# VectorE writes one element into both PSUM banks of a spectral step, and its eight products follow one another

## The chip, the cores and the metric

The kernel runs on one core of a Trainium2 chip. The metric is the device time of one execution in microseconds (us). TensorE is called PE in the profile, VectorE DVE, ScalarE ACT, GpSimd POOL, and SyncE SP; PEld is TensorE's loading of weights.

## What is computed

Eight sequences of 3072 positions and 256 channels pass three layers. The first is a filter in the frequency domain; the second and third are dense.

```python
X = np.fft.rfft(x, axis=1)                        # x: 8 x 3072 x 256, fp32
y = np.fft.irfft(X * (filt_r + 1j * filt_i), n=3072, axis=1)
prev = y shifted by one position
xk, xr = mu_k * y + (1 - mu_k) * prev, mu_r * y + (1 - mu_r) * prev
k = np.maximum(xk @ w_k, 0.0)                     # 256 -> 1024
z = sigmoid(xr @ w_r) * (k * k @ w_v)             # 1024 -> 256
h = np.maximum(np.maximum(z @ w1, z @ w2), z @ w3)  # 256 -> 768
out = h @ w_out                                   # 768 -> 256
```

## The kernel before

The **dense layers** are the main stream of the program. It takes 384 positions at a time. `k_mm` and `r_mm` multiply by `w_k` and `w_r`, `v_mm` by `w_v`; `block` does the maximum of three products for two such tiles at once with seven products in place of eight (tiles `pa`, `pb`, `pe`, line 850 on), and `o_mm` the last product (`po`). Each value is held as a sum of two parts, so that a product is three passes of 128x128 weights over 384 columns. ScalarE and VectorE read the banks out, and ScalarE, VectorE and GpSimd make the two parts.

The **transform** of sequence 0 runs ahead of all (`fft_first`). For sequences 1 to 7 `fft(b)` gives a list of small pieces, and `drive` deals them out among the main stream of the sequence before, by weight. A first part (`a_mm`, tile `pa<-xah,wa_s`) makes 24 groups of frequencies. The second part works on four groups at a time, so there are six values of `u` (`NU4`, line 29), and for each one `b_mm` (line 538: the transform's second stage, tile `pb<-xb,wbc`, then the filter) and one `c_mm` (line 559: the way back, tile `pc<-yz,wbc`). That is 12 steps for a sequence and 84 in all.

Each such **step** calls `quarters` (line 515). It takes two banks of the accumulator (PSUM) as `p[0]` and `p[1]`, and makes eight products with 64x64 weights over 256 columns. A product is named by `y`, `x` and `k`: `y` is the half of the 128 rows that the weights stand in, and also which of the two banks is written; `x` is the half of the columns and so of the bank's partitions; `k` is the half of the bank's 512 elements. The four places (`y`, `x`) of TensorE's array can work at the same time. A product is in full fp32, and the trace has two records of it, so that a step of eight products is 16 records.

All banks come from one **pool** of eight (`ps`, tag `pm`, line 261), for the main stream and the transform alike. A bank is taken again when its last reader is done, and whoever writes it first waits for that reader.

What sets the **order** on each engine: a scheduler plays the program through while it is built, with estimated times, and takes for an engine, of those instructions that it thinks ready, the one that stands first by priority. The products of `quarters` are written under `tc.high_priority()` and go ahead of the main stream as soon as the scheduler thinks them ready. Only the first part (`fft_first`, and SyncE's queue there) has an order by hand. On the chip each engine then works through its own fixed order, and waits on semaphores.

After `b_mm`'s products, for each bank: ScalarE copies the two halves of its partitions crosswise (lines 548, 549), VectorE multiplies by the filter (lines 550 to 552), and GpSimd does the rest (553, 555). After `c_mm`'s products ScalarE copies each bank out (line 566) and sends it to memory.

Of the kernel before, what the change touches and what calls it, by code (L numbers as in the profile page):

```python
# [11 lines left out]
I32 = mybir.dt.int32  # L12
U32 = mybir.dt.uint32
AF = mybir.ActivationFunctionType
ALU = mybir.AluOpType

N = 3072
# [12 lines left out]
H = NK // 2  # L30
# [175 lines left out]
def as_float(bits):  # L206
    return float(np.uint32(bits).view(np.float32))
# [29 lines left out]
def tile_spectral_moe(ctx: ExitStack, tc, x, xr, xz, filt, ones, wa, wa1, wi, wbc, wb1, wc1, filt1, filt0, mu, w_k, w_v, w_r, w1, w2, w3, w_out, out):  # L237
    nc = tc.nc
# [22 lines left out]
    ps = ctx.enter_context(tc.tile_pool(name="ps", bufs=8, space=bass.MemoryType.PSUM))  # L261

    def mm(o, wgt, rhs, start, stop, more=False, at=None):
        nc.tensor.matmul(o, lhsT=wgt, rhs=rhs, start=start, stop=stop, skip_group_check=more, tile_position=at)  # L264

    def mm3(o, parts, rhs_parts, onto=False, more=False):


        n = len(parts)
        for k in range(n):  # L270
            (wh, wl), (xh, xl) = parts[k], rhs_parts[k]
            mm(o, wh, xh, k == 0 and not onto, False, more)
            mm(o, wh, xl, False, False, more)
            mm(o, wl, xh, False, k == n - 1, more)
# [11 lines left out]
    def load_small():  # L286
        nc.scalar.dma_start(wi_s, wi)
        nc.scalar.dma_start(mu_s, mu)
        nc.vector.tensor_scalar(nmu_s, mu_s, -1.0, 1.0, op0=ALU.mult, op1=ALU.add)

    def split(hi, lo, src, lo_eng=None):
        nc.scalar.copy(hi, src)  # L292
        (lo_eng or nc.gpsimd).tensor_tensor(lo, src, hi.bitcast(F32), ALU.subtract)  # L293

# [3 lines left out]
    def piece(src, kt, t0, t1, c0, c1, parts):  # L298
# [18 lines left out]
        def narrow(late=True):  # L317
# [7 lines left out]
            ef = e.bitcast(F32)  # L325
            nc.scalar.activation(ef, high.bitcast(F32), AF.Abs)
            nc.vector.tensor_scalar(ef, ef, as_float(0x38000000), as_float(0x47EFFFFF), op0=ALU.max, op1=ALU.min)
            nc.vector.tensor_scalar(e, e, 3, 0x3FFFFFFF, op0=ALU.logical_shift_left, op1=ALU.bitwise_and)
            nc.vector.scalar_tensor_tensor(e, high, -0x40000000, e, ALU.bitwise_and, ALU.bitwise_or)
            m = fp.tile([P, a, c], I32, tag="fin", name="wm")  # L330
            mf = m.bitcast(F32)
            nc.vector.tensor_scalar(m, e, -0x800000, None, op0=ALU.bitwise_and)
            nc.vector.scalar_tensor_tensor(mf, low.bitcast(U32), 2.0**-52, mf, ALU.mult, ALU.mult)
# [106 lines left out]
    def fft(b):  # L440
# [73 lines left out]

        def quarters(o, of):

            for k in range(2):
                for y in range(2):
                    for x in range(2):
                        w, d = of(y, x, k)  # L520
                        with tc.high_priority():
                            mm(o[y][x * H : x * H + H, k], w, d, k == 0, True, True, (y * H, x * H))

        def b_load(u):
            w = fp.tile([NK, 2, 2, 2, H], F32, tag="fhi", name="wbc", bufs=3)
# [12 lines left out]
        def b_mm(u):  # L538
            w, f, t = st.pop(("b", u))
            p = [ps.tile([NK, 2, C], F32, tag="pm", name="pb") for _ in range(2)]  # L540
            quarters(p, lambda y, x, k: (w[y * H : y * H + H, 0, x, k], t[y * H : y * H + H, 2 * x + k]))
            y = []
            for z in range(2):
                fr, fi, q = f[z][:, 0], f[z][:, 1], p[z]
                v = fp.tile([NK, 2, C], F32, tag="flo", name="v", bufs=3)
                a, e, m = slice(0, NM), slice(NM, H), NM
                lo, hi = slice(H, H + NM), slice(H + NM, NK)
                nc.scalar.mul(v[lo], q[hi], sg_s[hi])
                nc.scalar.mul(v[hi], q[lo], sg_s[lo])
                nc.vector.scalar_tensor_tensor(fi[a], q[e], -1.0, fi[a], ALU.mult, ALU.mult)  # L550
                nc.vector.tensor_tensor(fi[e], q[a], fi[e], ALU.mult)
                nc.vector.tensor_tensor(fr, q, fr, ALU.mult)
                nc.gpsimd.tensor_tensor(fi[H:], v[H:], fi[H:], ALU.mult)
                yz = fp.tile([NK, 2, C], F32, tag="fin", name="yz")
                nc.gpsimd.tensor_tensor(yz, fr, fi, ALU.add)
                y.append(yz)
            st["c", u] = w, y

        def c_mm(u):
            w, t = st.pop(("c", u))  # L560
            p = [ps.tile([NK, 2, C], F32, tag="pm", name="pc") for _ in range(2)]
            quarters(p, lambda y, x, k: (w[y * H : y * H + H, 1, x, k], t[x][y * H : y * H + H, k]))
            sv = s2.rearrange("h m r g c -> (h m r) g c")
            for y in range(2):
                o = fp.tile([NK, 2, C], F32, tag="fo", name="co")
                nc.scalar.copy(o, p[y])
                g = 4 * u + 2 * y
                nc.scalar.dma_start(sv[:, g : g + 2, :], o)
# [211 lines left out]
    def r_mm(i):  # L780
        xh, xl = cs.pop(("r", i))
        g = mp.tile([P, 2, NT], F32, tag="gate", name="gate", bufs=3)
        for h in range(2):
            p = ps.tile([P, NT], F32, tag="pm", name="pr")
            s = slice(h * P, (h + 1) * P)
            mm3(p, [(wr[0][:, k, s], wr[1][:, k, s]) for k in range(2)], [(xh[:, k], xl[:, k]) for k in range(2)])
            nc.scalar.activation(g[:, h], p, AF.Sigmoid)
        cs["g", i] = g

    def k_mm(i, f):  # L790
# [4 lines left out]
        r = mp.tile([P, NT], F32, tag="kr", name="kr")  # L795
        nc.scalar.activation(r, p, AF.Relu)  # L796
        nc.vector.scalar_tensor_tensor(r, p, 0.0, r, ALU.max, ALU.mult)  # L797
# [247 lines left out]
    for p in range(1, NPAIR):  # L1045
        i = 2 * p + 2
# [85 lines left out]
```

## Time and profile before

| | us |
|---|---|
| time, median of 3 runs | 3199.36 (3198.39 to 3200.33) |
| the profiled execution | 3202.59 |
| its span, first to last instruction | 3200.7 |
| TensorE busy | 3119.8 (97%) |
| TensorE loading weights | 2966.4 (93%) |
| ScalarE busy | 1924.2 (60%) |
| VectorE busy | 1889.7 (59%) |
| GpSimd busy | 1740.4 (54%) |

The span is cut into stretches below: from 684 us to 850 us, for one, the steps of a sequence's transform run beside the main stream, and from 850 us to 1067 us there are none. This repeats some 383 us apart until 2766 us. The clock that TensorE was granted is given as a share of full speed. A timeline row gives the start, how long the row's merged instructions took from first start to last end, and their count; a matmul's record overlaps the next one's, so the distance of two starts, not the length, tells what a matmul takes from the engine's time. An entry in brackets at the end of a row is idle time ahead of it and what ended it.

### The profile page before, as it was taken

The numbers are of one execution on the slowest core, as the hardware profiler recorded it, in microseconds if no ns is written. First come the engines' busy times: TensorE is split into PE (matmuls) and PEld (weight loads), VectorE is DVE, ScalarE is ACT, GpSimd is POOL, SyncE is SP. The second block draws the span as 40 slices with busy tenths as digits, with TensorE's granted clock in tenths as the row PEclk, the third lists the DMA queues.
The fourth block names the chain that finished last, engine by engine and source line by source line (L and its number), as shares of the span: only waits on it lengthen the run. The fifth ranks groups of instructions, "written<-read, shape, count | busy, mean of one in ns | idle before, by whom it ended". The sixth has DMA issues, their size and how long they took to land.

```text
span 3200.7 us, 56204 instructions
## 1 busy us (share of the span) xinstructions
PE 3119.8 (97%) x19508; PEld 2966.4 (93%) x19508; DVE 1889.7 (59%) x3050; ACT 1924.2 (60%) x3968; POOL 1740.4 (54%) x1499
## 2 busy tenths in 40 slices
PE   6799999999999999999999999999999999999998
PEld 4799989999999999998999989999899999999998
DVE  4866666456665566555665466655665556555554
ACT  5556656566565565656666566665656566555554
POOL 3545655456564565545665455655655456444443
PEclk8799999999999999999999999999999999999999
DMA  9668667756777666856668576775777766555554
GB/s 293 225 219 283 201 221 251 205 172 206 242 237 201 189 199 211 268 174 201 218 216 242 168 221 202 255 215 166 225 222 242 197 180 204 172 172 159 167 167 122
DMA packets 388953, 666.64 MB, mean 208 GB/s; under 512 B 41760, under 2 KB 153408, under 8 KB 388032
## 3 DMA queue, kind: packets, MB, share of 16 engines
q1 hardware_dynamic: 323376, 588.23, 60.2%
q10 hardware_dynamic: 64576, 72.45, 6.5%
q8 instruction: 158, 2.59, 0.3%
q0 software_dynamic: 720, 2.36, 0.2%
q14 instruction: 123, 1.01, 0.1%
HBM read 577.03 MB, written 85.85 MB: 207 GB/s over the span
## 4 chain that ended last, share of the span: by engine, by line
PE 86%; DVE 6%; DMA 3%; ACT 2%; issue 2%; POOL 1%; SPq 0%; ACTq 0%; POOLq 0%; DVEq 0%
PE pb L264 20%; PE pk L264 13%; PE pv L264 13%; PE po L264 13%; PE pe L264 9%; PE pa L264 6%; PE pr L264 4%; PE py L264 4%; PE pc L264 2%; DVE sc L829 1%; DVE x L293 1%; PE ps L264 1%; DMA ws<-wud 1%; DVE kr L797 1%; POOL klo L293 1%
## 5 line engine op out<-in xcount | busy, mean ns | idle before, releaser
L264 PE MATMUL pb<-x,ws 128*128 128x384 f32 x3456 | 751.8, 338 | 3.8 <-DMA ws<-wud 2.3
L293 POOL TENSOR_TENSOR hh<-m,hh 128x384 fp32r<-128x384 f32 x384 | 407.2, 1069 | 616.6 <-ACT hh L292 509.7
L293 POOL TENSOR_TENSOR klo<-kr,khi 128x384 fp32r<-128x384 f32 x492 | 521.3, 1067 | 291.8 <-ACT khi L292 249.4
L264 PEld LDWEIGHTS pb<-x,ws 128*128 128x128 f32 x3456 | 598.4, 188 | 19.7 <-issue 8.4
L797 DVE SCALAR_TENSOR_TENSOR kr<-pk,kr 128x384 f32<-128x384 f32 x512 | 282.0, 553 | 451.8 <-ACT kr L796 450.4
L264 PE MATMUL pv<-khi,ws 128*128 128x384 f32 x2048 | 487.9, 340 | 13.5 <-ACT khi L292 13.4
L264 PE MATMUL po<-wo_hi,hh 128*128 128x256 f32 x2304 | 489.3, 284 | 2.7 <-ACT hh L292 2.0
L264 PEld LDWEIGHTS po<-wo_hi,hh 128*128 128x128 f32 x2304 | 392.1, 189 | 21.2 <-issue 9.6
L292 ACT CAST khi<-kr 128x384 fp32r<-128x384 f32 x512 | 262.1, 513 | 218.0 <-DVE kr L797 197.8
L264 PE MATMUL pe<-x,ws 128*128 128x384 f32 x1728 | 389.9, 338 | 0.0
L264 PEld LDWEIGHTS pv<-khi,ws 128*128 128x128 f32 x2048 | 361.6, 189 | 25.5 <-ACT khi L292 19.1
L264 PE MATMUL pk<-xh,wk_hi 128*128 128x384 f32 x1024 | 340.7, 337 | 3.9 <-ACT xh L292 3.3
L264 PE MATMUL pk<-xl,wk_hi 128*128 128x384 f32 x1024 | 344.3, 336 | 0.3 <-DVE xl L293 0.3
L264 PE MATMUL pk<-xh,wk_lo 128*128 128x384 f32 x1024 | 343.7, 336 | 0.0
L796 ACT ACTIVATE kr<-pk 128x384 f32<-128x384 f32 x512 | 249.6, 490 | 109.6 <-POOL klo L293 53.4
L264 PE MATMUL po<-wo_lo,hh 128*128 128x256 f32 x1152 | 315.5, 281 | 0.0
L264 PE MATMUL pv<-klo,ws 128*128 128x384 f32 x1024 | 305.5, 341 | 6.9 <-POOL klo L293 6.0
L264 PEld LDWEIGHTS pe<-x,ws 128*128 128x128 f32 x1728 | 298.2, 188 | 11.1 <-issue 9.6
L912 DVE TENSOR_TENSOR m<-sc,m 128x384 f32<-128x384 f32 x384 | 296.5, 775 | 8.1
L292 ACT CAST hh<-m 128x384 fp32r<-128x384 f32 x384 | 193.8, 514 | 152.6 <-DVE m L912 81.8
L293 POOL TENSOR_TENSOR xl<-xm,xh 128x768 fp32r<-128x768 f32 x126 | 231.3, 1854 | 91.6 <-ACT xh L292 91.5
L865 ACT COPY v<-pb 128x384 f32<-128x384 f32 x288 | 138.6, 481 | 175.7 <-PE pb L264 164.6
(129 smaller groups left out, 5777.1 us busy)
## 6 DMA issues: line engine op xcount, KB each, us to landing
ws<-wud SPq DMA_DIRECT2D x864, 256.0 KB, 3.4
ws<-wvd SPq DMA_DIRECT2D x512, 256.0 KB, 3.6
filt<-in_filt SPq DMA_DIRECT2D x84, 512.0 KB, 5.2
ws<-wud SPq DMA_DIRECT2D x288, 128.0 KB, 3.1
xz<-in_xz SPq DMA_DIRECT2D x56, 512.0 KB, 5.3
cin<-s SPq DMA_DIRECT2D x128, 192.0 KB, 4.3
out_dram<-osb ACTq DMA_DIRECT2D x192, 128.0 KB, 3.3
xr<-in_xr SPq DMA_DIRECT2D x56, 384.0 KB, 5.1
```

Of the source, the lines that this page charges most:

```text
L264: nc.tensor.matmul(o, lhsT=wgt, rhs=rhs, start=start, stop=stop, skip_group_check=more, tile_position=at)
L292: nc.scalar.copy(hi, src)
L293: (lo_eng or nc.gpsimd).tensor_tensor(lo, src, hi.bitcast(F32), ALU.subtract)
L796: nc.scalar.activation(r, p, AF.Relu)
L797: nc.vector.scalar_tensor_tensor(r, p, 0.0, r, ALU.max, ALU.mult)
L829: eng.tensor_tensor(t, a, b, ALU.subtract)
L865: nc.scalar.copy(st[to], st[of])
L912: nc.vector.tensor_tensor(m, c, m, ALU.max)
```

## The change

`mm` returns its instruction. `quarters` first has VectorE copy one element into each of the two banks, into the partition at which the row half `y` of the bank begins; the element comes from the data of that half's last product (`of(y, 1, 1)`), so that the copy also waits for that data. The second copy is kept behind the first. Then the eight products are made with `y` = 1 ahead of `y` = 0 for each `k`, and each is tied behind the one before it. `ORDER_ONLY` binds the scheduler's order and adds no semaphore. The copies stand outside of `tc.high_priority()`. The element that they write is overwritten by the products.

```diff
+ORDER_ONLY = mybir.DependencyInfo(mybir.DependencyClass.NoSync, mybir.DependencyReason.DATA)
@@
     def mm(o, wgt, rhs, start, stop, more=False, at=None):
-        nc.tensor.matmul(o, lhsT=wgt, rhs=rhs, start=start, stop=stop, skip_group_check=more, tile_position=at)
+        return nc.tensor.matmul(o, lhsT=wgt, rhs=rhs, start=start, stop=stop, skip_group_check=more, tile_position=at)
@@
         def quarters(o, of):
 
+            last = None
+            for y in range(2):
+                _, d = of(y, 1, 1)
+                i = nc.vector.tensor_copy(o[y][y * H : y * H + 1, 0, :1], d[:1, :1])
+                if y:
+                    tc.add_manual_dep(i.ins, last, ORDER_ONLY, reason="banks")
+                last = i.ins.name
+            last = None
             for k in range(2):
-                for y in range(2):
+                for y in (1, 0):
                     for x in range(2):
                         w, d = of(y, x, k)
                         with tc.high_priority():
-                            mm(o[y][x * H : x * H + H, k], w, d, k == 0, True, True, (y * H, x * H))
+                            i = mm(o[y][x * H : x * H + H, k], w, d, k == 0, True, True, (y * H, x * H))
+                        if last is not None:
+                            tc.add_manual_dep(i.ins, last, ORDER_ONLY, reason="quarters")
+                        last = i.ins.name
```

What this moves, first on TensorE, in a step of `b_mm` for sequence 2 (the names with a number are single tiles: `pb_7901` is the step's `p[0]`, `pb_7902` its `p[1]`; `pb1`, `pa1` and `pe1` are the main stream's banks). Before:

```order
L264 MATMUL pe1_7883<-x2_7560,ws_7805 128x384 [waits DMAHW0_49,DVE_49]
L264 MATMUL pe1_7883<-x2_7560,ws_7805 128x384 x2
L264 MATMUL pb_7901<-xb_7630,wbc_7628 64x256 [waits DVE_49]
L264 MATMUL pb_7901<-xb_7630,wbc_7628 64x256 x3
L264 MATMUL pb1_7831<-x2_7557,ws_7777 128x384 [waits Activation_49]
L264 MATMUL pb1_7831<-x2_7557,ws_7777 128x384 x2
L264 MATMUL pb_7902<-xb_7630,wbc_7628 64x256 [waits DVE_49]
L264 MATMUL pb_7902<-xb_7630,wbc_7628 64x256 x3
L264 MATMUL pb1_7875<-x2_7549,ws_7793 128x384 [waits Activation_49]
```

The four products of the first bank and the four of the second stand apart, with three products of the main stream between them. The same step on TensorE in the changed kernel (here `pb_7927` is `p[0]`, `pb_7928` is `p[1]`):

```order
L265 MATMUL pe1_7865<-x2_7590,ws_7811 128x384 [waits DVE_49]
L265 MATMUL pe1_7865<-x2_7590,ws_7811 128x384 x2
L265 MATMUL pb1_7901<-x2_7573,ws_7819 128x384 [waits Activation_49]
L265 MATMUL pb1_7901<-x2_7573,ws_7819 128x384 x2
L265 MATMUL pa1_7902<-x2_7576,ws_7842 128x384 [waits DMAHW1_49]
L265 MATMUL pa1_7902<-x2_7576,ws_7842 128x384 x2
L265 MATMUL pb1_7988<-x2_7566,ws_7866 128x384 [waits DMAHW3_49,Activation_49]
L265 MATMUL pb1_7988<-x2_7566,ws_7866 128x384 x2
L265 MATMUL pb_7928<-xb_7654,wbc_7652 64x256 [waits DVE_49]
L265 MATMUL pb_7928<-xb_7654,wbc_7652 64x256
L265 MATMUL pb_7927<-xb_7654,wbc_7652 64x256 x2
L265 MATMUL pb_7928<-xb_7654,wbc_7652 64x256 x2
```

The eight stand together now, and only the first waits. What it waits for is the second copy on VectorE, which stands in this place of VectorE's order (`gate` is `x2`'s product, `m` and `sc` belong to `block`):

```order
L916 TENSOR_TENSOR m_7871<-pe1_7865,v_7852 128x384 [waits Activation_49]
L830 TENSOR_TENSOR gate_7593<-pv_7705,gate_7593 128x384 [waits PE_49]
L830 TENSOR_TENSOR gate_7593<-pv_7706,gate_7593 128x384 [waits PE_49]
L521 COPY pb_7927<-xb_7654 1x1 [waits DMAHW0_49,DVE_49]
L521 COPY pb_7928<-xb_7654 1x1 [waits DMAHW4_49,DVE_49]
L923 TENSOR_TENSOR sc_7915<-pe1_7909,v_7894 128x384 [waits PE_49,Activation_49]
```

The two copies are new, and stand behind two additions to `gate` that do not belong to the step. The next step, one of `c_mm`, on VectorE (`pc_8083` is `p[0]`, `pc_8084` is `p[1]`):

```order
L521 COPY pc_8083<-yz_7689 1x1 [waits DVE_49]
L916 TENSOR_TENSOR m_8064<-pe1_8058,v_8032 128x384 [waits PE_49,Activation_49]
L924 TENSOR_TENSOR m_7871<-sc_8002,m_7871 128x384 [waits DVE_49]
L521 COPY pc_8084<-yz_7689 1x1 [waits Activation_49]
L920 TENSOR_TENSOR m_8018<-pa1_8051,m_8018 128x384 [waits PE_49]
```

and on TensorE:

```order
L265 MATMUL pb1_8050<-x2_7581,ws_7971 128x384 [waits Activation_49]
L265 MATMUL pb1_8050<-x2_7581,ws_7971 128x384 x2
L265 MATMUL pe1_8058<-x2_7590,ws_7990 128x384 [waits DVE_49]
L265 MATMUL pe1_8058<-x2_7590,ws_7990 128x384 x2
L265 MATMUL pc_8084<-yz_7680,wbc_6480 64x256 [waits DVE_49]
L265 MATMUL pc_8084<-yz_7689,wbc_6480 64x256
L265 MATMUL pc_8083<-yz_7680,wbc_6480 64x256
```

Two instructions of the main stream stand between the two copies here, and three products of `pe1_8058` between the read of `pe1_8058` by `m_8064` and the step. Over the whole program, TensorE's order before has the eight products of a step in two pieces of four in 42 of the 84 steps (six of each sequence's twelve); in 26 more they stand together, all four of one bank ahead of all four of the other, and in 16 together with the banks mixed. In the changed kernel they stand together in all 84. VectorE has 168 instructions more.

## Rows read from the trace of the kernel before

**Rows 1.** Page, busy time by engine, and granted clock in 40 slices.

```profile
PE 3119.8 (97%) x19508; PEld 2966.4 (93%) x19508; DVE 1889.7 (59%) x3050; ACT 1924.2 (60%) x3968; POOL 1740.4 (54%) x1499
...
PEclk8799999999999999999999999999999999999999
```

**Rows 2.** Busy time by stretch, with steps (684, 1067) and without (850).

```profile
core 0: us, PE busy (x) PEld busy (x) DVE busy (x) ACT busy (x) POOL busy (x), PEclk, DMA share, GB/s
...
684.00:850.00 166.00, 163.91 (x1073) 148.71 (x1072) 104.83 (x169) 104.62 (x208) 97.08 (x83) 1.00 0.67 210
850.00:1067.00 217.00, 216.90 (x1343) 214.22 (x1343) 122.73 (x201) 132.96 (x283) 121.52 (x105) 1.00 0.70 214
1067.00:1232.00 165.00, 162.91 (x1067) 147.72 (x1067) 104.90 (x167) 103.67 (x208) 96.84 (x82) 1.00 0.67 210
```

**Rows 3.** Timeline of TensorE, a step in two pieces: start, us, engine, operation, count.

```profile
708.88 0.69 PE L264 MATMUL pe<-x,ws 128*128 128x384 f32 x3
709.49 1.08 PE L264 MATMUL pb<-xb,wbc 64*64 64x256 f32 x8
710.50 0.79 PE L264 MATMUL pb<-x,ws 128*128 128x384 f32 x3
711.22 1.08 PE L264 MATMUL pb<-xb,wbc 64*64 64x256 f32 x8
712.23 0.79 PE L264 MATMUL pb<-x,ws 128*128 128x384 f32 x3
712.86 0.33 PE L264 MATMUL pa<-x,ws 128*128 128x384 f32 x1
```

**Rows 4.** Timeline of TensorE, a step together, one bank's four products first.

```profile
350.65 0.68 PE L264 MATMUL pe<-x,ws 128*128 128x384 f32 x3
351.17 0.68 PE L264 MATMUL pb<-x,ws 128*128 128x384 f32 x3
351.79 1.11 PE L264 MATMUL pb<-xb,wbc 64*64 64x256 f32 x16
352.82 0.38 PE L264 MATMUL po<-wo_hi,hh 128*128 128x256 f32 x1
353.05 0.28 PE L264 MATMUL po<-wo_lo,hh 128*128 128x256 f32 x1
353.17 0.28 PE L264 MATMUL po<-wo_hi,hh 128*128 128x256 f32 x1
```

**Rows 5.** Timeline of TensorE, a step together, banks mixed.

```profile
377.09 0.34 PE L264 MATMUL pk<-xl,wk_hi 128*128 128x384 f32 x1
377.35 1.10 PE L264 MATMUL pc<-yz,wbc 64*64 64x256 f32 x16
378.38 0.44 PE L264 MATMUL pk<-xh,wk_lo 128*128 128x384 f32 x1
378.66 0.33 PE L264 MATMUL pk<-xh,wk_hi 128*128 128x384 f32 x1
```

**Rows 6.** Timeline of TensorE, the first and the last of 42 steps in pieces.

```profile
367.93 1.08 PE L264 MATMUL pb<-xb,wbc 64*64 64x256 f32 x8
...
369.60 1.08 PE L264 MATMUL pb<-xb,wbc 64*64 64x256 f32 x8
...
2757.99 1.08 PE L264 MATMUL pc<-yz,wbc 64*64 64x256 f32 x8
...
2763.66 1.08 PE L264 MATMUL pc<-yz,wbc 64*64 64x256 f32 x8
```

**Rows 7.** Waits of TensorE, 684 to 850 us: total, times, longest.

```profile
PE pv L264 <- ACT khi L292: 1.3, 1, 1.3
PE pv L264 <- POOL klo L293: 0.8, 1, 0.8
```

**Rows 8.** Timeline of TensorE, the one step ahead of which it waited.

```profile
409.96 0.65 PE L264 MATMUL pc<-yz,wbc 64*64 64x256 f32 x4 [0.46 <-DVE filt L552]
412.07 1.98 PE L264 MATMUL pc<-yz,wbc 64*64 64x256 f32 x12 [1.46 <-DVE filt L552]
```

**Rows 9.** Groups of VectorE: count, busy us, mean ns, idle before.

```profile
L912 DVE TENSOR_TENSOR m<-sc,m 128x384 f32<-128x384 f32 x384 | 296.5, 775 | 8.1
...
L289 DVE TENSOR_SCALAR nmu_s<-mu_s 128x4 f32<-128x4 f32 x1 | 0.2, 169 | 7.4 <-DMA mu_s<-in_mu 7.4
```

**Rows 10.** Timeline of VectorE ahead of the step in rows 3.

```profile
707.37 1.02 DVE L818 TENSOR_TENSOR gate<-pv,gate 128x384 f32<-128x384 f32 x2 [3.43 <-PE pv L264]
708.31 0.55 DVE L908 TENSOR_TENSOR m<-pa,m 128x384 f32<-128x384 f32 x1
708.77 0.55 DVE L904 TENSOR_TENSOR m<-pe,v 128x384 f32<-128x384 f32 x1
```

## Prediction

> **What bounds the kernel now.** I read the busy times first. TensorE is busy for 97% of the span, the others for 54 to 60%, and its granted clock is full after the first slices [rows 1]. The stretches tell whether that holds where the change works: beside a transform TensorE is busy for 163.9 of 166 us, and without one for 216.9 of 217 [rows 2]. So it is TensorE's own order that sets the end, in both kinds of stretch, and in a stretch with twelve steps only about 2.1 us of waiting are to be had, 1.3 and 0.8 us on the main stream's `pv` products [rows 7]. None of it is a wait of the steps. What a step takes of TensorE's time is therefore worth its full length at the end of the program, up or down.
>
> The timelines of TensorE then give the price of a step. The reader has to look at distances of starts. A plain product takes 0.173 us (three from 350.65 to 351.17) and a `po` product 0.12 (353.05 to 353.17) [rows 4].
>
> - In two pieces [rows 3]: from 708.88 to 712.86 there are two pieces of four products (8 records each) and nine plain ones. 3.98 - 9 x 0.173 = 2.42 us, so 1.21 us a piece. That includes what is lost at its edges: 0.61 us from 708.88 to 709.49 for three plain products where 0.52 is usual, and as much again behind it.
> - Together [rows 4]: from 351.17 to 353.05 there are three plain products, the 16 records and one `po`. 1.88 - 0.52 - 0.12 = 1.24 us.
> - Together with the banks mixed [rows 5]: from 377.09 to 378.66, two plain products and 16 records. 1.57 - 0.35 = 1.22 us.
>
> So four products cost as much as eight. The eight run on four places of the array, two places for each `y`, and a piece has one `y` alone: half of the array stands idle in it.
>
> **The change, part by part.**
>
> *Joining the pieces.* Before, 42 of the 84 steps are in two pieces, the first and the last of them in [rows 6]. Each goes from 2.42 to 1.24 us, which gives 1.18 us, and 42 x 1.18 = 49.6 us. The changed order has all 84 together. The order inside the eight is a new one, with `y` = 1 first and two by two. Two other orders differ by 0.02 us [rows 4, 5], so I take nothing for that; 42 x 0.02 = 0.8 us bounds it. The 42 steps that were together already stay what they are.
>
> The Trainium skill says otherwise of one thing: TensorE: Matmul & The Clock Gate, Part 3, The mechanism, has matmuls start and end in strict program order. By that rule the order in the step told first, four of one `y` and then four of the other, would take as long as two pieces, and the 26 such steps would gain from the new order as well. The trace disagrees: 16 records of that order took 1.11 us from first start to last end [rows 4], no longer than the mixed ones' 1.10 [rows 5].
>
> *The copies.* 84 x 2 = 168 new instructions of VectorE on one element. The trace has none like them. The nearest row is the 128x4 operation with 169 ns [rows 9], which I take: 168 x 0.169 = 28.4 us of VectorE's time. VectorE is busy for 104.8 of 166 us where they fall [rows 2], so 24 x 0.169 = 4.1 us a stretch find room in its own time. From below the cost at the end is nothing, if TensorE has other work while they run; from above it is the whole 28.4, if TensorE stands through each of them.
>
> The Trainium skill has a rule against such copies: VectorE: DVE Perf Modes, Two Vector instructions with no wait between them, holds back an instruction whose partitions begin in another quadrant until all earlier ones are done. In the trace neighbours on VectorE do overlap, 708.31 and 708.77 start 0.46 us apart and take 0.55 each [rows 10]; with that 0.09 lost at each copy it would be 168 x 0.26 = 43.7 us of VectorE's time. No run here shows a copy held in this way.
>
> *The new wait.* Before, the first product of each bank waited for that bank's last reader. Now the eight wait for the second copy, and that for all that stands ahead of it on VectorE, which is strictly in order. The price is what VectorE needs from its last meeting with TensorE to the copy, less what TensorE has to do in the same time. In the first step shown, `m_7871` must be done before `pe1_7865`'s last three products. TensorE then has twelve plain products ahead of the step, 12 x 0.173 = 2.08 us. VectorE has two additions to `gate`, 1.02 us together [rows 10], and two copies, 0.34 us: 1.36 us, covered with 0.7 to spare. In the second step, after `m_8064` TensorE has three products, 0.52 us, plus the 0.09 at the edge. VectorE has an `m` of 0.55 to 0.78 us [rows 9, 10] and one copy of 0.17, together 0.72 to 0.95: TensorE stands for 0.1 to 0.3 us. I went through the twelve steps of this sequence in the changed order in this way: nine are covered with 0.3 us or more, two come out even, and one is the step just told. That is 0.1 to 0.5 us for a sequence, 7 x 0.3 = 2 us in all. Where a copy waits for ScalarE to free a bank, the order does not tell how late that is; I allow as much again. Together 4 us.
>
> Queued behind a waiting copy on VectorE is the main stream: `m`, `sc`, `kr`. ScalarE and then TensorE wait for these. VectorE's cover for that is the 61 us it is idle in a stretch of 166.
>
> *The banks.* The first bank is now taken, and stays empty, until the second is free as well. Before, its four products ran meanwhile. That costs nothing as long as the main stream finds enough of the other six banks, and the scheduler has placed main-stream products there; in the second step shown, two instructions of VectorE stand between the two copies. The other edits (the return value, the binding without a semaphore) add no instruction.
>
> *The sum.* The profiled execution took 3202.6 us. 3202.6 - 49.6 + 4 = 3157.0. It stands 3.2 us above the median of the runs, 3199.4, so for the median I take 3153.8, and forecast 3154.
>
> **The rivals.**
>
> *VectorE comes late throughout.* The scheduler's estimate of VectorE is too short, and TensorE stands for both copies at every step. Then all of the 28.4 us are lost: 3199.4 - 49.6 + 28.4 = 3178. For it speaks that the first product had to wait for nothing like this before; against it that in all the steps shown but the one told next [rows 8] TensorE never stood ahead of a step, though those waits were placed by the same scheduler.
>
> *The banks run short, and the kernel is slower.* TensorE stands while a first bank is kept for its partner. The place is the 42 steps that were in pieces, whose second bank came late: 1.73 us after the first in one of them (709.49 to 711.22) [rows 3], 5.67 in the last [rows 6]. If TensorE stood for the smaller of these in each, 42 x 1.73 = 72.7 us would be lost: 3199.4 - 49.6 + 72.7 = 3222.5. It is slower than before from 49.6 / 42 = 1.18 us a step on. For it speaks the one step in the trace that TensorE stood for, 0.46 and 1.46 us [rows 8]; against it that VectorE and ScalarE have 40% of idle time to free banks in, and that TensorE's changed order has plain products ahead of each step.
>
> *The eight don't run side by side.* They stand together in the order, but a product with `y` = 0 starts only when those with `y` = 1 are done, so that a step costs two pieces less two edges. Edges are some 0.2 us of a piece; 42 x 0.2 = 8.4 us would be won and about 4 lost to waits, and the 42 steps that are together now would lose: 42 x 0.98 = 41 us, as 2.42 - 0.2 - 1.24 = 0.98. That is 3236. Neither of the two orders of the eight in the trace did this [rows 4, 5].
>
> *The program-order rule holds after all,* and 26 more steps gain 1.18 us each: 30.7 us more, 3123. The trace is against it [rows 4].
>
> *A wash:* waits of 0.5 to 0.65 us a step over all 84, from VectorE's queue and from banks together, take 42 to 55 us, and the time stays within 0.2% (6.4 us, about what a measurement of this kernel can tell from no change).
>
> **How the numbers follow.** Forecast 0.76; VectorE late throughout 0.13; a wash 0.04; banks short 0.04; the eight not side by side 0.02; program-order rule 0.01. The forecast's own range is 3144 to 3164: up by 10 us of waits more, down by the waits that may go, 2 us of each stretch and 3.5 us around the step that waited [rows 8]. To leave out no more than 2 in 10 the range goes up to the rival with VectorE's copies and the 4 us on top of it: 3144 to 3182. Faster by over 0.2%: 0.76 + 0.13 + 0.01 = 0.90. Same 0.04. Slower 0.06.
>
> **What would show it.** The timelines after should have no piece with 8 records of `wbc`, and 84 rows with 16 that take 1.1 us; TensorE's busy time should fall by some 50 us, to about 3070, with its instructions unchanged, and its idle time in a stretch with steps should stay below 4 us. VectorE's groups should have 168 copies with a mean under 0.2 us. If the forecast fails by waits, rows of `wbc` carry a bracket with the copy's line behind the arrow (VectorE late) or the main stream's do with the readers of banks (banks short). If a row of 16 takes 2 us, the eight don't run side by side. The forecast rests most on TensorE's waits staying small: 0.6 us a step would undo it.

## The result, and the profile after

The changed kernel takes 3170.09 us (median of four runs, 3169.33 to 3171.45), and the kernel before, beside it, 3199.79 us (3198.39 to 3200.33). The ratio is 0.9913, 95% interval 0.9900 to 0.9925: 29.7 us faster. The forecast was 3154, so the sign is right and the time is 16 us above it. It lies inside the stated range, 3144 to 3182, but 6 us above the forecast's own range, 3144 to 3164; only the part that was added for the rival "VectorE comes late throughout" takes it in.

The page's busy times of the changed kernel, to be read against [rows 1]:

```profile
PE 3073.5 (97%) x19508; PEld 2938.0 (93%) x19508; DVE 1910.6 (60%) x3218; ACT 1913.8 (60%) x3968; POOL 1746.8 (55%) x1499
```

Its profiled execution took 3169.33 us with a span of 3167.4, 33.3 us less than before. TensorE's busy time fell by 46.3 us, and its idle time rose from 3200.7 - 3119.8 = 80.9 us to 3167.4 - 3073.5 = 93.9: 13.0 us came back as waits. 46.3 - 13.0 = 33.3.

The step that stood in two pieces in [rows 3] now reads so in TensorE's timeline (start, us, engine, operation, count):

```profile
700.10 0.69 PE L265 MATMUL pb<-x,ws 128*128 128x384 f32 x3
700.72 1.09 PE L265 MATMUL pb<-xb,wbc 64*64 64x256 f32 x16
701.74 0.79 PE L265 MATMUL pb<-x,ws 128*128 128x384 f32 x3
702.37 0.52 PE L265 MATMUL pe<-x,ws 128*128 128x384 f32 x2
```

Sixteen records stand in one row. From 700.10 to 702.37 there are six plain products and the step: 2.27 - 6 x 0.173 = 1.23 us, where the pieces took 2.42. Over all 84 steps the distances of starts give 1.225 us a step, and before 1.210 for a piece and 1.237 for a step together. (Here and below, a step is priced by the distance of starts around it, less the usual distance for the plain products in between, as the median over the steps.) So the change frees 42 x (2 x 1.210 - 1.225) + 42 x 0.012 = 50.7 us of TensorE's time.

The groups of the copies and of the products behind them (count, busy us and mean ns, idle time ahead and what ended it):

```profile
L521 DVE COPY pc<-yz 1x1 f32<-1x1 f32 x84 | 13.0, 155 | 2.7
L521 DVE COPY pb<-xb 1x1 f32<-1x1 f32 x84 | 13.0, 155 | 27.8 <-ACT gate L799 22.9 <-ACT co L578 1.5 <-ACT osb L950 1.1
...
L265 PE MATMUL pb<-xb,wbc 64*64 64x256 f32 x672 | 46.0, 389 | 0.5 <-DVE pb L521 0.5
L265 PE MATMUL pc<-yz,wbc 64*64 64x256 f32 x672 | 46.0, 389 | 0.5 <-DVE pc L521 0.5
```

The copies take 26.0 us of VectorE's time, and TensorE stood ahead of a step for 0.5 + 0.5 = 1.0 us in all, at two of the 84 steps. The waits that came back are in other places. TensorE's waits over the whole program (total us, times, longest), of which [rows 7] had one stretch:

```profile
PE pv L265 <- ACT khi L293: 12.3, 17, 2.9
PE pv L265 <- POOL klo L294: 10.5, 9, 1.6
...
PE pb L265 <- ACT v L877: 4.2, 6, 0.7
...
PE pv L265 <- DVE pc L521: 1.8, 1, 1.8
```

The same view of the kernel before:

```profile
PE pv L264 <- ACT khi L292: 13.4, 10, 2.9
...
PE pv L264 <- POOL klo L293: 6.0, 10, 0.8
```

All of these are waits of the main stream's products: for `klo` and `khi`, the two parts of `k` that GpSimd and ScalarE make, and for ScalarE to empty a `pb` bank (line 877). Those for `klo` grew by 4.5 us, those for `v` are new, and those for `khi` fell by 1.1. One wait of 1.8 us ended with a copy of a step, once, in the first sequence (388 us); before that copy VectorE had stood 1.31 us for the filter's data from memory. By stretch, the one with steps and the one without, against [rows 2], with the same columns:

```profile
675.00:833.00 158.00, 155.74 (x1067) 144.94 (x1069) 106.47 (x188) 100.82 (x204) 96.68 (x82) 1.00 0.69 219
833.00:1055.00 222.00, 220.57 (x1353) 215.03 (x1345) 124.28 (x205) 135.04 (x287) 122.85 (x106) 1.00 0.69 211
```

TensorE idles 2.26 us in the first (2.09 before) and 1.43 us in the second (0.10 before). The stretch without steps got the larger share, though 0.70 us of it is the wait for `v` shown below, which comes just behind the last step. Two places show what such a wait is. At 787 us two additions `yz` of the transform stand ahead of `klo` on GpSimd:

```profile
781.88 1.09 PE L265 MATMUL pc<-yz,wbc 64*64 64x256 f32 x16
...
787.26 2.52 POOL L567 TENSOR_TENSOR yz<-filt 128x512 f32<-128x512 f32 x2
789.75 1.95 POOL L294 TENSOR_TENSOR klo<-kr,khi 128x384 fp32r<-128x384 f32 x2
...
790.79 0.61 PE L265 MATMUL pv<-klo,ws 128*128 128x384 f32 x2 [1.57 <-POOL klo L294]
```

The same place in the kernel before:

```profile
795.28 1.10 PE L264 MATMUL pc<-yz,wbc 64*64 64x256 f32 x16
...
800.76 2.54 POOL L555 TENSOR_TENSOR yz<-filt 128x512 f32<-128x512 f32 x2
803.25 1.99 POOL L293 TENSOR_TENSOR klo<-kr,khi 128x384 fp32r<-128x384 f32 x2
804.32 0.62 PE L264 MATMUL pv<-klo,ws 128*128 128x384 f32 x2 [0.78 <-POOL klo L293]
```

GpSimd has the same work there in both, and `klo` comes as late: the product starts 8.9 us after the step ahead of it, and 9.0 us before the change. That step stood together before the change too, so it got no shorter. What differs is what TensorE has in between: 34 plain products after and 40 before, 6 x 0.173 = 1.04 us less, and the wait is 0.79 us longer. The same wait stands in six sequences, nearly equal in each, which makes 6 x 0.79 = 4.7 us. So here the wait grew because the new order has fewer products between the step and `klo`.

The other place is just behind the sequence's last step, where ScalarE has two banks of the step and a bank of `block` to empty:

```profile
832.31 1.09 PE L265 MATMUL pc<-yz,wbc 64*64 64x256 f32 x16
833.33 0.97 PE L265 MATMUL pb<-x,ws 128*128 128x384 f32 x4
833.49 1.07 ACT L578 COPY co<-pc 128x512 f32<-128x512 f32 x2 [3.22 <-PE pc L265]
834.45 0.50 ACT L877 COPY v<-pb 128x384 f32<-128x384 f32 x1
835.00 0.79 PE L265 MATMUL pb<-x,ws 128*128 128x384 f32 x3 [0.70 <-ACT v L877]
```

The two copies of `pc` now fall due together, `v` stands behind them, and TensorE waits 0.70 us for it. This is the wait for `v` in the table, in six sequences.

### The profile page after: what moved, and what is told of

It reads as the page before. It is cut to its first block, busy times and chain, and to the rows that moved or that the text cites. A ratio compares the mean times of both kernels' runs of the same rounds, so it can differ in the third digit from the quotient of the medians.

```text
span 3167.4 us, 56436 instructions
## 1 busy us (share of the span) xinstructions
PE 3073.5 (97%) x19508; PEld 2938.0 (93%) x19508; DVE 1910.6 (60%) x3218; ACT 1913.8 (60%) x3968; POOL 1746.8 (55%) x1499
## 5 line engine op out<-in xcount | busy, mean ns | idle before, releaser
L294 POOL TENSOR_TENSOR hh<-m,hh 128x384 fp32r<-128x384 f32 x384 | 414.2, 1088 | 634.8 <-ACT hh L293 513.1
L265 PE MATMUL pv<-khi,ws 128*128 128x384 f32 x2048 | 480.8, 339 | 14.9 <-ACT khi L293 12.3
L265 PE MATMUL pv<-klo,ws 128*128 128x384 f32 x1024 | 298.7, 340 | 13.6 <-POOL klo L294 10.5
```

What stands on the lines that cost most here:

```text
L265: return nc.tensor.matmul(o, lhsT=wgt, rhs=rhs, start=start, stop=stop, skip_group_check=more, tile_position=at)
```

## The experiments

All edits are to the changed kernel, unless said. The kernel before took 3198.29, 3197.82 and 3197.13 us beside the three groups of runs (first four, next four, last four). The last column but one needs a word: *waits* are TensorE's distances of starts beyond the usual ones, summed over all rows after the first 300 us (those hold the transform of sequence 0, which the change does not touch). They hold the short waits too, which the profile counts as busy time, and what a lower granted clock costs: in the kernel before TensorE was granted 0.50 (1.2 in place of 2.4 GHz) from 411.7 to 418.5 us, after it had begun to wait 1.46 us ahead of a step [rows 8], and the plain products there took some 2 us longer; after has no such stretch between 121 us and the last 10 us. Each figure is from one profiled execution. That of e10_before_klo, 3224.77 us, was the fastest of four whose median is 3238.84.

| kernel | us | ratio, 95% interval | steps in two pieces | a step's price, us | waits | span |
|---|---|---|---|---|---|---|
| before | 3199.79 | 1 | 42 | 2.420 / 1.237 | 52.7 | 3200.7 |
| after | 3170.09 | 0.9913 (0.9900 to 0.9925) | 0 | 1.225 | 74.6 | 3167.4 |
| e1_ties | 3201.57 | 1.0010 (1.0000 to 1.0019) | 52 | 1.99 in pieces | 62.5 | 3195.5 |
| e2_copies | 3200.23 | 1.0005 (0.9996 to 1.0015) | 41 | 2.420 / 1.237 | 55.2 | 3196.2 |
| e3_halves | 3168.38 | 0.9903 (0.9888 to 0.9918) | 0 | 1.238 | 71.3 | 3166.1 |
| e4_between | 3253.60 | 1.0172 (1.0157 to 1.0187) | 84 | 2.452 | 55.2 | 3250.2 |
| e5_scalar | 3191.64 | 0.9983 (0.9973 to 0.9992) | 0 | 1.224 | 96.4 | 3189.7 |
| e6_wide | 3172.02 | 0.9924 (0.9909 to 0.9939) | 0 | 1.224 | 76.5 | 3171.0 |
| e7_evac | 3166.37 | 0.9904 (0.9890 to 0.9919) | 0 | 1.225 | 73.7 | 3165.5 |
| e8_early | 3167.76 | 0.9904 (0.9889 to 0.9918) | 0 | 1.225 | 70.4 | 3165.4 |
| e9_klo | 3205.34 | 1.0027 (1.0016 to 1.0038) | 0 | 1.225 | 109.9 | 3203.3 |
| e10_before_klo | 3238.84 | 1.0121 (1.0100 to 1.0142) | 40 | 2.424 / 1.233 | 80.3 | 3223.0 |
| e11_both | 3163.54 | 0.9891 (0.9874 to 0.9907) | 0 | 1.225 | 69.8 | 3161.7 |
| e12_klo_both | 3195.16 | 0.9995 (0.9986 to 1.0004) | 0 | 1.224 | 96.3 | 3195.1 |

The books of before and after in this measure: 50.7 us freed, and 21.9 us more waits after the first 300 us and 3.1 less before, 18.8 in all. That leaves 31.9, and the spans differ by 33.3. The 3.1 us are not the change's: no step stands in the first 300 us, and e3_halves, which differs from the changed kernel only inside the eight, reaches the same place of TensorE's order (matmul record 1400) at 309.15 us, as before does (309.23), where after reaches it at 306.00. So what came back where the change works is about 21.9 us, less what else differs between two executions.

### Which part of the change does it: ties, copies, order

The first theory was that the returned waits come with the copies, the rival that they come with any new order of the main stream.

**e1_ties**: the ties alone.

```diff
-            for y in range(2):
-                _, d = of(y, 1, 1)
-                i = nc.vector.tensor_copy(...)
-                if y:
-                    tc.add_manual_dep(i.ins, last, ORDER_ONLY, reason="banks")
-                last = i.ins.name
```

> The eight products are tied as in the change, and VectorE writes nothing. In the built order 52 steps stand in two pieces, 32 together. Theory (a step in two pieces costs 1.19 us more; the 16 us that the change won less than forecast went to waits that come with VectorE's copies): ten pieces more than before and waits as before, 3199.8 + 10 x 1.19 = 3212 us. Rival (those 16 us come with any new order of the main stream): 3170 + 52 x 1.19 = 3232 us.

It came to 3201.57, and neither number held. Without the copies the ties do not keep a step together: 52 of the 84 are in two pieces, now of two products and of six. TensorE's timeline (columns as above):

```profile
703.25 0.65 PE L265 MATMUL pb<-xb,wbc 64*64 64x256 f32 x4
703.83 0.79 PE L265 MATMUL pb<-x,ws 128*128 128x384 f32 x3
704.46 0.70 PE L265 MATMUL pa<-x,ws 128*128 128x384 f32 x3
705.09 1.08 PE L265 MATMUL pb<-xb,wbc 64*64 64x256 f32 x12
```

Two products cost 0.78 us and six 1.21, 1.99 together, where I had priced pieces at 2.42. So the copies are needed to keep the eight together. The single records show why six cost what four do: in a piece of four, all of one `y`, records start in pairs at 0, 0.27, 0.48 and 0.70 us, and in a piece of six or a step of eight up to four records start at each of the same four times. The price goes by the half `y` that has the most products.

**e2_copies**: the copies alone, with the eight products in the order of before and untied.

```diff
-                for y in (1, 0):
+                for y in range(2):
@@
-                        if last is not None:
-                            tc.add_manual_dep(i.ins, last, ORDER_ONLY, reason="quarters")
-                        last = i.ins.name
```

> VectorE's copies as in the change, the products in the order of before and not tied. In the built order 41 steps stand in two pieces, one less than before. Theory (the waits come with the copies): 3199.8 - 1 + 16 = 3215 us. Rival (the waits come with a new order, and go either way): 3199 us, give or take 5.

3200.23, and the rival held. All 168 copies are there, 41 steps are still in pieces, and the waits are 55.2 us, 2.5 above before's. The copies by themselves bring no time and cost none to speak of.

**e3_halves**: all four products of `y` = 1, then all four of `y` = 0.

```diff
-            for k in range(2):
-                for y in (1, 0):
+            for y in (1, 0):
+                for k in range(2):
```

> The change with another order inside the eight: all four of y = 1, then all four of y = 0. All 84 steps stand together. Theory (the order inside does not matter): 1.22 us a step as in the change, 3170 us, give or take 5 for other waits of the main stream; that scatter is what this run is also for. Rival (products start in program order, so that one half runs after the other): 2.2 us a step, 3170 + 84 x 1.0 = 3254 us.

3168.38: as the changed kernel. A row of 16 records is 1.11 us long, as [rows 4] and [rows 5] had it. Four records start within 0.04 us at the head of a step, though a piece of one half has only two there; so products of `y` = 0 start beside the first ones of `y` = 1 and ahead of its last ones. The order inside the eight is worth nothing.

**e4_between**: e3_halves with one plain product of 128x128 weights over 64 columns between the two halves; its result is overwritten by the step.

```diff
+                        if y == 0 and k == 0 and x == 0:
+                            with tc.high_priority():
+                                i = mm(o[0][:, 0, :64], wk[0][:, 0, :P], wk[0][:, 0, :64], True, True, True)
+                            tc.add_manual_dep(i.ins, last, ORDER_ONLY, reason="quarters")
+                            last = i.ins.name
```

> As the run with the four of one half ahead of the other's, and between the halves one more product with 128x128 weights over 64 columns, whose result is overwritten. So every step is in two pieces with the same waits ahead. Theory (a piece of four costs what eight do, 1.21 us, the product between 0.1): 84 x (2.42 + 0.1 - 1.22) = 109 us more than the change, 3279 us. Rival (joining the pieces is not what won the time; a piece costs half of a step plus the 0.2 us at its edges): 84 x 0.3 = 25 us more, 3195 us.

3253.60, between the two: the theory had the step's price about right (2.452 us for 2.52), and left out the waits. TensorE's timeline:

```profile
719.51 0.70 PE L265 MATMUL pe<-x,ws 128*128 128x384 f32 x3
720.14 1.08 PE L265 MATMUL pc<-yz,wbc 64*64 64x256 f32 x8
721.16 0.30 PE L265 MATMUL pc<-wk_hi 128*128 128x64 f32 x1
721.38 1.08 PE L265 MATMUL pc<-yz,wbc 64*64 64x256 f32 x8
722.39 0.79 PE L265 MATMUL pb<-x,ws 128*128 128x384 f32 x3
```

One product of another shape between the halves puts them one behind the other again. Copies, ties and banks are those of e3_halves; the step's price differs, 2.452 us for 1.238, and the main stream's order around the steps is planned anew. That is 84 x 1.214 = 102 us more of TensorE's time, but the span grew by 84.1 us. The other 18 us are waits that went: 16.1 after the first 300 us, and 1.4 before, where no step stands. TensorE's waits of e3_halves:

```profile
PE pv L265 <- ACT khi L293: 11.2, 16, 2.9
PE pv L265 <- POOL klo L294: 10.5, 9, 1.6
PE pb L265 <- ACT v L877: 4.3, 6, 0.7
```

and of e4_between:

```profile
PE pv L265 <- ACT khi L293: 8.2, 9, 3.8
PE pv L265 <- POOL klo L294: 6.7, 8, 1.0
PE pb L265 <- ACT v L882: 4.1, 6, 0.7
```

The waits for `khi` and `klo` fall when TensorE is given more to do, and that for `v` stays. So the first theory fell: with the same copies 16 us less are lost. For `klo` the place shown above tells how. In e4_between it reads:

```profile
798.08 1.08 PE L265 MATMUL pc<-yz,wbc 64*64 64x256 f32 x8
...
806.99 0.62 PE L265 MATMUL pv<-klo,ws 128*128 128x384 f32 x2 [0.99 <-POOL klo L294]
```

The product again starts 8.9 us after the step's start, as in e3_halves (783.55 and 792.44 us), so `klo` is no sooner. The step is 1.21 us longer, three plain products fewer stand behind it (31 for 34, 0.52 us), and the wait fell from 1.6 to 1.0 us, in each of six sequences. So a longer step does take from this wait, and a step made shorter just ahead of it would add to it. That is 6 x 0.6 = 3.6 of the 16 us; the rest was not traced in this way, and a part of it may be the new order's, since orders planned anew differ by some 4 us (below).

### Who is late: the copies, the banks, ScalarE

**e5_scalar**: ScalarE writes the two elements. **e6_wide**: VectorE copies 256 elements in place of one.

```diff
-                i = nc.vector.tensor_copy(o[y][y * H : y * H + 1, 0, :1], d[:1, :1])
+                i = nc.scalar.copy(o[y][y * H : y * H + 1, 0, :1], d[:1, :1])       # e5_scalar
+                i = nc.vector.tensor_copy(o[y][y * H : y * H + 1, 0, :], d[:1, :])  # e6_wide
```

> The change with ScalarE writing the two elements in place of VectorE. All 84 steps stand together. Theory A (the waits lost come from VectorE's queue, behind which the step and the main stream stand): most of the 16 us come back, 3156 us, unless ScalarE's queue takes over. Theory B (they come with a new order of the main stream): 3170 us, give or take 5.

> The change with each copy of 256 elements in place of one; the trace of the change has a copy at 0.155 us, this should take about 0.25 us more. Theory A (VectorE's copies lie on TensorE's path): up to 168 x 0.25 = 42 us more, 3212 us; already half of it, 3191 us, would tell. Theory B (they are covered): 3170 us, give or take 5.

e5_scalar: 3191.64, 21.6 us slower than with VectorE. No theory had this number; theory A had only named ScalarE's queue as its exception. ScalarE's copies are as short, 152 ns, and the steps cost the same. But a copy that waits holds up what stands behind it. In the groups (idle time ahead behind the second bar), VectorE's `kr` waits 28.2 us for ScalarE because of line 521, and in TensorE's waits `khi` and `klo` are higher than in the changed kernel:

```profile
L809 DVE SCALAR_TENSOR_TENSOR kr<-pk,kr 128x384 f32<-128x384 f32 x512 | 280.0, 553 | 452.9 <-ACT kr L808 423.7 <-ACT pb L521 28.2
```

```profile
PE pv L265 <- ACT khi L293: 16.3, 24, 3.3
PE pv L265 <- POOL klo L294: 14.6, 8, 2.2
```

The clock takes a part too. Five of these waits for `klo` are 2.2 us long (in the changed kernel 1.6 at most), and behind each TensorE's granted clock fell to 0.50 (1.2 in place of 2.4 GHz). The wait that ended at 798.2 us was followed by this stretch (columns as in [rows 2]):

```profile
799.40:802.80 3.40, 3.40 (x12) 3.40 (x11) 0.00 (x0) 1.38 (x4) 1.00 (x1) 0.50 0.95 352
```

Each costs some 1.5 us, by the distances of starts in it, 7.5 us for the five. The changed kernel's trace has none of them.

e6_wide: 3172.02, 1.9 us slower. Its copies, in the groups:

```profile
L521 DVE COPY pc<-yz 1x256 f32<-1x256 f32 x84 | 35.4, 421 | 2.9 <-issue 0.3
L521 DVE COPY pb<-xb 1x256 f32<-1x256 f32 x84 | 35.3, 421 | 29.0 <-ACT gate L799 25.9 <-ACT osb L950 0.8
```

They take 70.7 us where the short ones took 26.0: 44.7 us more of VectorE's time cost 1.9 at the end. So the length of the copies is covered. Which engine's queue they wait in is not indifferent.

**e7_evac**: VectorE copies out the second bank of `c_mm`, so that ScalarE has one of the two. **e8_early**: the copies too go under high priority, so that VectorE meets them sooner.

```diff
-                nc.scalar.copy(o, p[y])
+                (nc.vector.tensor_copy if y else nc.scalar.copy)(o, p[y])           # e7_evac
@@
-                i = nc.vector.tensor_copy(o[y][y * H : y * H + 1, 0, :1], d[:1, :1])
+                with tc.high_priority():                                            # e8_early
+                    i = nc.vector.tensor_copy(o[y][y * H : y * H + 1, 0, :1], d[:1, :1])
```

> The change with the second bank of c_mm copied out by VectorE in place of ScalarE. Theory C (both banks of a step end together now, ScalarE copies both in a row for 1.07 us, and a copy of the main stream behind them comes late; the 0.87 us at 835 us in the trace, once for each sequence): 7 x 0.87 = 6 us less, 3164 us. Theory B (new order): 3170 us, give or take 5.

> The change with the copies under the same high priority as the products, so that they take the banks as early as they can be had and VectorE does them ahead of the main stream's work. Theory D (a first bank that stands empty costs the main stream): the bank is held longer or as long, 3170 us or more, up to 3190. Theory A (the step waits for what stands ahead of the copies on VectorE): less ahead of them, 3160 us. Theory B: 3170 us, give or take 5.

e7_evac: 3166.37. The six waits for `v` fell from 4.2 us to 1.3, but one new wait of a step, 3.4 us, came in their stead; TensorE's waits:

```profile
PE pb L265 <- ACT v L877: 1.3, 6, 0.2
PE pc L265 <- DVE pc L521: 3.9, 2, 3.4
```

The 3.7 us gained have the size that orders which were only planned anew differ by (3168 to 3172 in e3_halves, e6_wide and e8_early), so this fits the cause and does not prove it. e8_early: 3167.76. A copy that comes sooner keeps its bank longer empty, and it cost nothing; but the mean time from the first copy's end to the products went only from 2.83 to 2.92 us, so this tests the banks weakly.

### Can the chain be shortened

If TensorE's arrival at `klo` is what costs, a shorter way to `klo` should give more after the change than before. Both kernels got the same edit: VectorE makes `klo` for every odd block of 128 columns, in all tiles, where GpSimd made nearly all.

```diff
-        split(hi, lo, r, nc.vector if i == 0 or i < 4 and f % 2 else None)
+        split(hi, lo, r, nc.vector if i == 0 or f % 2 else None)
```

> The change with the second part of every other kr (klo, odd f) made by VectorE in place of GpSimd, in all tiles and not in the first four alone: 0.69 us in place of 1.08 on the main stream's chain from pk to pv. Theory E (TensorE, 50 us quicker in the steps, now runs into the main stream's chains of ScalarE, VectorE and GpSimd, which are as long as ever; pv<-klo waits are 18.5 us here and 12.8 in the kernel before): the shorter chain takes away a good part of the klo waits, 3160 us. Theory B (a new order goes either way): 3170 us, give or take 5.

> The kernel before with the same move of klo to VectorE. 40 of its 84 steps stand in two pieces. Theory E: TensorE arrives later there, so that the shorter chain is worth less than in the change: 3195 us, at most half of what it gives there. Theory B: no tie between the two, 3198 us, give or take 5.

Both lost, 35 us after the change (3205.34) and 42 us before it (3238.84, to 3197.13 beside it), where a gain was expected. 240 of the 512 `klo` moved, and in e9_klo VectorE is busy for 2099.8 us in place of 1910.6. One takes 0.81 us there, where 0.69 had been assumed, and VectorE's own queue is now in the way. TensorE's waits of e9_klo:

```profile
PE pk L265 <- DVE filt L564: 15.1, 6, 2.5
...
PE pv L265 <- DVE klo L294: 10.7, 10, 2.1
PE pb L265 <- DMA ws<-wud: 10.1, 8, 3.4
```

The wait for `klo` is hardly shorter (10.7 us, and 0.6 for those that GpSimd still makes, in place of 10.5 and 1.7), `pk` has a new one of 15.1 us behind the filter's operations, and `pb` one of 10.1 us for weights from memory. The pair says nothing of the cause, since the edit did not shorten the chain. That VectorE is idle for 40% does not mean that it can be given anything: these operations were not covered.

**e11_both** is e7_evac and e8_early together, **e12_klo_both** is that with the edit to `klo`.

> The change with both of the edits that came out quickest: the second bank of c_mm copied out by VectorE, and VectorE's copies under high priority. They gave 3.7 and 2.3 us apart; if both are real and add up, 3164 us; if they are scatter of a new order, 3164 to 3172 us.

> All three edits: klo of odd f on VectorE, the second bank of c_mm on VectorE, the copies under high priority. Theory E: 3155 us. Theory B: 3168 us, give or take 5. If VectorE becomes too full (it is 60% busy in the change, this adds some 240 x 0.69 us = 166 us, 5%, and 42 x 0.6 = 25 us), 3175 us or more.

e11_both: 3163.54, the fastest kernel of this study, 6.5 us (0.2%) below the changed one, and 1.1% below before (0.9891, 0.9874 to 0.9907). It does not decide between the two expectations, which both begin at 3164. In e12_klo_both `klo` on VectorE costs 31.6 us again (3195.16). The page of e11_both:

```profile
PE 3076.9 (97%) x19508; PEld 2943.1 (93%) x19508; DVE 1924.0 (61%) x3260; ACT 1895.6 (60%) x3926; POOL 1747.1 (55%) x1499
```

It is faster by idle time alone: 3161.7 - 3076.9 = 84.8 us, against 93.9. The waits for `klo` are not among what fell, with 11.4 us in place of 10.5.

## Why the prediction was right in sign and 16 us too low

By its steps:

- *What bounds the kernel.* Right: a step's price went to the end of the program, less the waits told below. e4_between shows it the other way round, 84 us of 102.
- *Joining the pieces.* Right: 49.6 us forecast, 50.7 measured (2 x 1.210 to 1.225 a step). All 84 are rows of 16 records.
- *The order inside the eight.* Right: nothing, by e3_halves. The rival by the program-order rule, 3123, falls with it: the single records of e3_halves show products of one half starting ahead of earlier ones of the other. In the mixed order and in the other the eight cost 1.225 and 1.238 us.
- *The copies.* Right: 0.155 us each (estimated 0.169), covered. The rule on held copies in the Trainium skill (VectorE: DVE Perf Modes, Two Vector instructions with no wait between them) would have made them 0.26 us of VectorE's time each, by the prediction's estimate. The trace of the changed kernel agrees, against the prediction's remark that no run shows it. Of the 168 copies none starts before the operation ahead of it on VectorE has ended, and nothing starts before a second copy has ended; elsewhere 1419 of 2916 neighbours overlap by 0.05 us or more. Where two copies follow each other directly, the pair takes 0.40 us from the end of the operation ahead to the start of the next, where an overlap of 0.08 us is usual: 0.24 us each. The record, 0.155, does not show it. It did not matter for the end: e6_wide lengthened each copy by 0.27 us for 1.9 us in all.
- *The new wait* is the step that failed: the 4 us. I looked for it in the wrong place, at the meetings of VectorE and TensorE at the twelve steps; there the waits came to 1.0 us, or 2.8 with the one of `pv` that ended with a copy, less than I allowed. What I put at nothing without a reason is what a new order of the main stream does to the rest: the waits for `klo` grew, because six products fewer stand ahead of them, and the banks of `c_mm` fall to ScalarE two at once, ahead of `v`. In the profiled executions the term measured 13.0 us of idle time; with the short waits that lie in busy time it is 18.8 over the whole program, and 21.9 where the change works.
- *The banks.* Nothing was forecast, and no run contradicts it, but none puts it to a hard test.
- *The sum.* 3170.1 - 3153.8 = 16.3 us: 9.0 are the waits (13.0 in place of 4), 3.3 are TensorE's busy time (46.3 less in place of 49.6, for the short waits in it), and 4.0 are the step from the profiled execution to the median. I took 3.2 us off, because before's lay so far above its median; after's lies 0.8 below its own. These 4.0 us are chance of two executions and no step of the argument; 3.1 us of the difference between the two lie in the first 300 us.

Of the rivals, VectorE late throughout (3178) is the nearest in time, 8 us off. But its mechanism isn't there: TensorE stood for a copy at a step for 1.0 us, not 28. That the stated range held the result is owed to this rival, and so to luck. The wash rested on waits at the steps, the banks too; neither came.

What came back is settled in part. By main-stream tile, the distances of starts grew by 9.4 us ahead of `pb`, 7.4 ahead of `pv` and 3.3 ahead of `pe`. Shown is that it is neither the copies' work (e2_copies, e6_wide) nor the order of the eight (e3_halves); that the 4.7 us more at `klo` come with the new order, since the step ahead of that place was together before the change too; and that a longer step takes from the same wait (e4_between, 0.6 us a sequence). Whether the freed time itself, apart from the order, brought back any of the rest stays open: every comparison here has a new order in it. The burst at the two banks of `c_mm` is seen in the trace and shrinks with e7_evac, but its gain of 3.7 us is not clear of the scatter of orders planned anew, some 4 us. Whether keeping an empty bank costs anything stays open too. A run with the old order of the main stream around the joined steps, or with more room between the making of `klo` and its use, would test it; neither was run.

## What to carry to other kernels

Price a saving on the engine that sets the end by distances of starts, and then give part of it back: in this case 18.8 to 21.9 of 50.7 us, some 40%, returned as waits, not at the changed place but where that engine meets chains of the others that were just in time, or where the new order leaves less to do ahead of them. Look ahead of a prediction for waits that are already there, however short (1.3 and 0.8 us in a stretch, [rows 7]), and for readers that will now fall due together. A short instruction that only orders things belongs on an engine whose queue can stand still at that moment: the same copy cost 21.6 us more on ScalarE than on VectorE. Idle share is no measure of room: 240 operations moved to VectorE, idle for 40%, cost 35 us.

## What was new of the hardware

- A run of 64x64 products between products of 128x128 is priced by the half of the rows that has the most of them, and what the other half does beside it is nearly free: two products of one half 0.78 us, four of one half 1.21, four of one and two of the other 1.21, four of each 1.225 to 1.238.
- One plain product over 64 columns between two fours undoes this: 2.452 us for the step (e4_between).
- A copy of one element into the accumulator takes 0.155 us on VectorE and 0.152 on ScalarE; 256 elements of one partition take 0.421 us on VectorE.
